# A layernorm feeding a diagonal state-space layer and a Mish MLP: the pipeline rebuilt around one PSUM accumulation, with B and C resident on chip, sine tables and one ring for the weights

## The chip, the core and the metric

The kernel runs on one core of one Trainium2 chip. The metric is the device time of one execution in microseconds (us), taken as the median of several runs; lower is better. In the text PE is the tensor engine (matmuls), DVE the vector engine, ACT the scalar engine (functions by table), POOL the general engine, SP the engine whose queue only issues transfers. Each engine works through its own instructions in order; semaphores tie them together.

## The reference, cut to what matters

```python
xn = layernorm(x)                                   # x: (2048, 1024), bf16
# A: a diagonal state-space layer with 1024 complex channels
dt = exp(log_dt);  Lam_bar = exp(dt * Lam)
Bu = xn @ (((Lam_bar - 1) / Lam)[:, None] * B).T    # complex, (2048, 1024)
h[t] = Lam_bar * h[t - 1] + Bu[t]                   # over the 2048 rows
yA = 2 * real(h @ C.T) + xn * Dskip
# B: a Mish MLP
u  = xn @ w1 + b1                                   # (2048, 3584)
yB = (u * tanh(log(1 + exp(u)))) @ w2               # softplus in the stable form
out = x + yA + yB
```

## The kernel before

The 2048 rows are cut into 4 blocks of 512. A block has four stretches of matmuls, each matmul 128 x 128 weights against 512 columns. `but_block` (the input projection): 8 channel groups j, each real and imaginary, 8 contraction steps k: 128 matmuls on line 761. `ffn1_block` (dense 1): 28 tiles f of 128 hidden units, 8 steps each: 224 matmuls on line 714. `tail_block`: dense 2, 28 tiles f into 8 PSUM banks (4 row tiles q times 2 column halves): 224 on line 801; then the output projection, 8 groups j, two parts, into the same banks: 128 on line 818.

The rows are normalized by DVE with one square root on ACT per row tile (`ln_tile` for block 0, lines 387 to 406, with two buffers; `mln_*` for the later blocks), stored to a scratch in DRAM (line 405 or 612) and read back transposed, eight transfers of 128 columns (`dma_xnT`, line 419). B is read transposed at the start, 16 transfers on SP (line 473) under one semaphore, so the first matmul waits for all of them. C is read transposed again in every block (`dma_rs`, line 463). w1 and w2 stream in every block through two sets of three slots (lines 443 and 452); a transfer waits on SP until PE has read the slot.

The recurrence is made a plain running sum: the projected input is multiplied by tables Wt that hold the inverse powers of Lam_bar (lines 767 to 778), summed along the row axis (lines 658 and 661), and multiplied by Vt, the powers with the factor of C (lines 681 to 692). The tables are built on DVE by nine doublings (lines 531 to 551); Vt is built in pieces between the bias adds of dense 1 in block 0 (`deferred`, lines 558 to 573). Four one-element instructions per group carry the state to the next block (lines 667 to 680).

Mish runs by groups of 7 tiles: DVE adds the bias out of PSUM (line 719), ACT does Exp, Ln and Tanh tile by tile (727, 732, 737) with table loads between, and POOL multiplies (739). POOL also loads row tiles of x and of the scratch again (626, 628) and forms x + xn * Dskip (634, 637); DVE adds that to the PSUM banks and ACT issues the stores (825 to 832).

What sets the order is the position in each engine's list, and for each instruction the waits that `_hazards` derives from the buffers it reads and writes. Block order in `build_kernel`: `but_block`, `ffn1_block`, `tail_block`.

## Time and profile before

| | us |
|---|---|
| runs, in order | 780.35, 2398.21, 777.31 |
| median of the runs | 780.35 |
| span of the profiled execution | 777.7 |
| granted clock of PE, mean over the span | 0.968 |
| PE busy, DVE busy | 627.5, 568.8 |
| ACT busy, POOL busy | 261.0, 274.0 |

The profiled execution is known by its span, from its first to its last instruction; what lies around it isn't shown for it, and the span lies between the two lower runs. One of the three runs took three times as long; the median leaves it aside.

How to read the profile: a row of a group gives line, engine, operation, the tile written and the tiles read, shapes and count, then the busy time and the mean duration (ns) of one, then how long the engine sat idle just before these instructions and what ended most of that. A row of the chain of waits or the timeline begins with the time from the span's start and a duration in us. A row of a stage gives for PE, the weight loads, DVE, ACT and POOL the busy us and the number of instructions, then PE's granted clock, the busy share of the DMA engines and GB/s. Matmuls are pipelined: their mean duration is longer than the time from one to the next.

### The profile page before, as it was taken

The numbers are of one execution on the slowest core, as the hardware profiler recorded it, in microseconds if no ns is written. First come the engines' busy times: TensorE is split into PE (matmuls) and PEld (weight loads), VectorE is DVE, ScalarE is ACT, GpSimd is POOL, SyncE is SP. The second block draws the span as 40 slices with busy tenths as digits, with TensorE's granted clock in tenths as the row PEclk, the third lists the DMA queues.
The fourth block names the chain that finished last, engine by engine and source line by source line (L and its number), as shares of the span: only waits on it lengthen the run. The fifth ranks groups of instructions, "written<-read, shape, count | busy, mean of one in ns | idle before, by whom it ended". The sixth has DMA issues, their size and how long they took to land.

```text
span 777.7 us, 8473 instructions
## 1 busy us (share of the span) xinstructions
PE 627.5 (81%) x2760; PEld 277.6 (36%) x2816; DVE 568.8 (73%) x1018; ACT 261.0 (34%) x415; POOL 274.0 (35%) x276
## 2 busy tenths in 40 slices
PE   0000999567998699898999787999999699999992
PEld 0000444223443244343444333444444244444441
DVE  2599999960599879738997289549995198479932
ACT  0250004599000000799400000999100005994000
POOL 0000000546344410146745310345664300567653
PEclk9999999997999899999999989999999999999997
DMA  4279014268568761454569913354669804514372
GB/s 55 75 176 168 0 55 139 79 189 191 194 228 180 150 142 55 136 148 123 181 216 171 211 62 108 110 152 145 206 171 179 169 8 137 160 60 172 116 144 81
DMA packets 193019, 105.70 MB, mean 136 GB/s; under 512 B 112464, under 2 KB 173904, under 8 KB 192976
## 3 DMA queue, kind: packets, MB, share of 16 engines
q1 hardware_dynamic: 183376, 86.28, 44.3%
q0 software_dynamic: 4992, 14.69, 6.9%
q10 hardware_dynamic: 4608, 4.20, 1.9%
q8 instruction: 23, 0.38, 0.2%
q14 instruction: 20, 0.16, 0.1%
HBM read 71.58 MB, written 8.39 MB: 103 GB/s over the span
## 4 chain that ended last, share of the span: by engine, by line
PE 26%; DVE 22%; DMA 16%; POOL 14%; ACT 12%; SPq 5%; issue 4%; POOLq 0%; DVEq 0%; ACTq 0%
PE bank L714 15%; DMA xntf<-bass_xn_scratch 11%; PE bank L761 8%; ACT actT L737 4%; POOL xdsk L634 4%; POOL actT L739 4%; POOL xdsk L637 4%; ACT actT L732 3%; SPq L473 3%; ACT actT L727 2%; DVE stats L590 2%; PE bank L801 2%; DVE hb L719 2%; DMA xl<-in_A_x_dram 2%; POOL xtf L626 2%
## 5 line engine op out<-in xcount | busy, mean ns | idle before, releaser
L739 POOL TENSOR_TENSOR actT<-hb,actT 128x512 bf16<-128x512 bf16 x112 | 141.8, 1301 | 357.3 <-ACT actT L737 324.2
L801 PE MATMUL bank<-w2s,actT 128*128 128x512 bf16 x880 | 199.7, 386 | 15.5 <-issue 6.1
L714 PE MATMUL bank<-xnT,w1s 128*128 128x512 bf16 x876 | 196.3, 381 | 19.3 <-DVE hb L719 18.3
L761 PE MATMUL bank<-xnT,BT 128*128 128x512 bf16 x504 | 117.8, 394 | 92.6 <-DMA BT<-in_A_B_im_dram 76.8
L727 ACT ACTIVATE actT<-hb 128x512 bf16<-128x512 bf16 x112 | 62.8, 618 | 330.2 <-DVE hb L719 329.7
L801 PEld LDWEIGHTS bank<-w2s,actT 128*128 128x128 bf16 x896 | 88.5, 99 | 126.4 <-issue 17.6
L714 PEld LDWEIGHTS bank<-xnT,w1s 128*128 128x128 bf16 x896 | 87.1, 98 | 127.9 <-issue 21.3
L719 DVE TENSOR_SCALAR hb<-bank,b1col 128x512 bf16<-128x512 f32 x112 | 81.0, 747 | 58.4 <-PE bank L714 40.6
L818 PE MATMUL bank<-rhs,hT 128*128 128x512 bf16 x500 | 115.5, 389 | 9.2 <-DVE hT L691 8.6
L761 PEld LDWEIGHTS bank<-xnT,BT 128*128 128x128 bf16 x512 | 51.1, 101 | 158.6 <-DMA BT<-in_A_B_im_dram 76.8
L634 POOL TENSOR_TENSOR xdsk<-xntf,dsk 128x512 bf16<-128x512 bf16 x32 | 42.5, 1328 | 104.1 <-DMA xntf<-bass_xn_scratch 104.1
L818 PEld LDWEIGHTS bank<-rhs,hT 128*128 128x128 bf16 x512 | 50.8, 100 | 73.2 <-DVE hT L691 10.6
L825 DVE TENSOR_TENSOR outs<-bank,xdsk 128x512 bf16<-128x512 f32 x32 | 20.9, 687 | 71.0 <-PE bank L818 32.0
L732 ACT ACTIVATE actT<-actT,consts 128x512 bf16<-128x512 bf16 x112 | 70.3, 708 | 0.2
L737 ACT ACTIVATE actT<-actT 128x512 bf16<-128x512 bf16 x112 | 60.0, 616 | 0.2
L637 POOL TENSOR_TENSOR xdsk<-xdsk,xtf 128x512 bf16<-128x512 bf16 x32 | 41.3, 1291 | 4.6
L661 DVE TENSOR_TENSOR_SCAN cum<-zeros,qb,hT 128x512 bf16<-128x512 bf16 x24 | 40.4, 1682 | 0.0
L590 DVE BATCH_NORM_STATS2 stats<-xl_60 128x6 f32<-128x512 bf16 x24 | 16.5, 689 | 32.5 <-DMA xl_60<-in_A_x_dram 32.1
L658 DVE TENSOR_TENSOR_SCAN cum<-zeros,qb,hT 128x512 bf16<-128x512 bf16 x24 | 34.2, 1426 | 0.0
L727 ACT ACT_TABLE_LOAD x3 | 3.8, 1283 | 71.1 <-PE bank L761 71.0
L767 DVE TENSOR_TENSOR mtmp<-bank,Wt 128x512 bf16<-128x512 f32 x32 | 22.1, 690 | 3.0
L773 DVE TENSOR_TENSOR mtmp<-bank,Wt 128x512 bf16<-128x512 f32 x32 | 22.1, 692 | 1.1
(113 smaller groups left out, 481.2 us busy)
## 6 DMA issues: line engine op xcount, KB each, us to landing
w1s<-in_B_w_dram SPq DMA_DIRECT2D x56, 512.0 KB, 3.8
w2s<-in_B_w_dram SPq DMA_DIRECT2D x56, 512.0 KB, 3.7
xtf<-in_A_x_dram POOLq DMA_DIRECT2D x32, 128.0 KB, 3.4
xntf<-bass_xn_scratch POOLq DMA_DIRECT2D x32, 128.0 KB, 3.5
out_dram<-outs ACTq DMA_DIRECT2D x32, 128.0 KB, 4.1
xl_60<-in_A_x_dram POOLq DMA_DIRECT2D x12, 256.0 KB, 4.7
bass_xn_scratch<-xnl_61 POOLq DMA_DIRECT2D x12, 256.0 KB, 5.0
xl<-in_A_x_dram SPq DMA_DIRECT2D x4, 256.0 KB, 2.7
```

Source lines behind the costliest of these rows:

```text
L634: pop(lambda e, bb_=bb_, xs=xs, u=u: e.tensor_tensor(xdsk[:, u, :], xntf[:, xs, :], dsk[:, bb_ * TB:(bb_ + 1) * TB], op=ALU.mult), reads=[ ...
L637: pop(lambda e, xs=xs, u=u: e.tensor_tensor(xdsk[:, u, :], xdsk[:, u, :], xtf[:, xs, :], op=ALU.add), reads=[b_xtf[xs], b_xdsk[u]], writes ...
L661: vop(lambda e, cim_=cim_, vim=vim, init_im=init_im: e.tensor_tensor_scan(out=cim_, data0=zeros[:], data1=vim, initial=init_im, op0=ALU.ad ...
L714: return e.matmul(banks[bank][:, :], lhsT=w1s[:, s_, k, fi * P128:(fi + 1) * P128], rhs=xnT[:, k, :], start=(k == 0), stop=(k == NK - 1))
L719: vop(lambda e, hs=hs, bank=bank, f=f: e.tensor_scalar(hb[:, hs, :], banks[bank][:, :], b1col[:, f:f + 1], None, op0=ALU.add), reads=[b_ba ...
L727: aop(lambda e, hs=hs, f=f: e.activation(actT[:, f, :], hb[:, hs, :], AF.Exp), reads=[b_hb[hs]], writes=[b_act[f]])
L732: aop(lambda e, ff=ff: e.activation(actT[:, ff, :], actT[:, ff, :], AF.Ln, bias=consts[:, 2:3], scale=1.0), reads=[b_act[ff], b_consts], w ...
L737: aop(lambda e, ff=ff: e.activation(actT[:, ff, :], actT[:, ff, :], AF.Tanh), reads=[b_act[ff]], writes=[b_act[ff]])
L739: pop(lambda e, hs2=hs2, ff=ff: e.tensor_tensor(actT[:, ff, :], hb[:, hs2, :], actT[:, ff, :], op=ALU.mult), reads=[b_hb[hs2], b_act[ff]], ...
L761: return e.matmul(banks[bk][:, :], lhsT=BT[:, ci, k, j * P128:(j + 1) * P128], rhs=xnT[:, k, :], start=(k == 0), stop=(k == NK - 1))
L801: return e.matmul(banks[u][:, :], lhsT=actT[:, f, q * P128:(q + 1) * P128], rhs=w2s[:, s_, fi, bb_ * TB:(bb_ + 1) * TB], start=first, stop ...
L818: return e.matmul(banks[u][:, :], lhsT=hT[:, ci, j, q * P128:(q + 1) * P128], rhs=rhs[:, s_, ci, bb_ * TB:(bb_ + 1) * TB], start=False, st ...
```

## The change

The kernel is written anew around the same four stretches of matmuls; the matmuls are as many and as large as before.

- Order in a block: dense 1, then the input projection, then dense 2 and the output projection in one accumulation (`tail`). The first 6 tiles of dense 2 go to banks 4 to 7 first. The last three groups of the output projection go row tile by row tile, so that the adds and stores of the first row tile begin before the last matmuls.
- Layernorm: x is loaded once, kept in `xx`; the normalized rows stay in `xn`. For block 0 they are transposed by PE into PSUM and copied out; for later blocks by transfers from on-chip memory (`transpose_dma`). The scratch in DRAM is gone. DVE forms x + xn * Dskip in place (`ln_skip`) and adds the PSUM banks to it.
- The recurrence uses the scan with a decay r = |Lam_bar| on DVE; the rotation is taken off before it and put on after it with cosine and sine tables (`tab`). Tables: POOL computes phases less whole turns, ACT takes Sin. Products work on real and imaginary parts in one instruction.
- B and C are read transposed once, during dense 1 of block 0, on SP, between the ring's loads; C is scaled by the channels' factor on ACT and DVE in block 0 (`scale_C`).
- w1 and w2 share one ring of 7 slots of 512 KB in the order of use.
- Mish: Exp, Ln and Tanh are one instruction for 7 tiles, and the product is one DVE instruction (`mish_mul`) in place of 7 on POOL.
- Parameter vectors are loaded row-wise by POOL and transposed by PE.

The core of the diff (the helper classes are rewritten too; waits are derived in the same way):

```diff
-    xn_scr = nc.dram_tensor("bass_xn_scratch", (S, D), bf16).ap()
-    NW2S = 3
-    w2s = sb("w2s", [P128, NW2S, 2, D], bf16); b_w2s = [Buf("w2s%d" % i) for i in range(NW2S)]
-    NRS = 4
-    NW1S = 3
-    w1s = sb("w1s", [P128, NW1S, NK, 256], bf16); b_w1s = [Buf("w1s%d" % i) for i in range(NW1S)]
...
+    NRING = 7
+    ring = sb("ring", [P, NRING, 2048], bf16)
+    CT = sb("CT", [P, 2, NJ, D], bf16)
...
+    ph = [scratch("ph_%s%d" % w, w[0], w[1], f32, TB)
+          for w in (("h", 2), ("h", 3), ("h", 6), ("h", 7), ("a", 11), ("a", 12), ("a", 13),
+                    ("h", 0), ("h", 1), ("h", 4), ("h", 5))]
...
-    def dma_xnT(c_):
-        for k in range(NK):
-            def fn(e, c_=c_, k=k):
-                return e.dma_start_transpose(xnT[:, k, :], xn_scr[c_ * TB:(c_ + 1) * TB, k * P128:(k + 1) * P128])
-            dma(fn, s_xnT, reads=[b_xnscr[c_ * NQ + q_] for q_ in range(NQ)], writes=[b_xnT])
...
-    def dma_rs(c_, j):
-        if c_ >= NB or (c_, j) in rs_done:
...
+    items = []
+    for blk in range(NB):
+        items += [("w1", g) for g in range(NF // 2)] + [("w2", g) for g in range(NF // 2)]
...
+        kind, g = items[i]
+        s = i % NRING
+        if kind == "w1":
+            dst = ring[:, s, :].rearrange("p (k f) -> p k f", k=NK)
+            src = B_w1[:, g * 256:(g + 1) * 256].rearrange("(k p) f -> p k f", p=P)
...
+    def ln_stats(blk, q):
+        i, s = blk % 2, q % 2
+        for h in range(2):
+            vop(lambda e, h=h: e.bn_stats(stats[:, s, h, :], xx[:, i, q, h * 512:(h + 1) * 512]),
...
+        aop(lambda e: e.activation(rs[:, q, 1:2], rs[:, q, 0:1], AF.Sqrt), reads=[b_rs[q]], writes=[b_rs[q]])
+    def ln_apply(blk, q):
+        i = blk % 2
...
+        vop(lambda e: e.tensor_scalar(xn[:, q, :], xx[:, i, q, :], mv[:, q, 0:1], y,
+                                      op0=ALU.subtract, op1=ALU.mult),
+    def ln_skip(blk, q):
+        i = blk % 2
...
+        vop(lambda e: e.tensor_tensor(m, xn[:, q, :], dsk[:], op=ALU.mult),
...
+        vop(lambda e: e.tensor_tensor(xx[:, i, q, :], xx[:, i, q, :], m, op=ALU.add),
...
+    def transpose_dma(q):
+        SP.dma(lambda e: e.dma_start_transpose(xnT[:, :, q * P:(q + 1) * P], xn[:, q, :]),
...
+    for q in range(NQ):
+        ln_stats(0, q)
+        if q:
+            ln_apply(0, q - 1)
+    ln_apply(0, NQ - 1)
+    for q in range(NQ):
+        for k in range(NK):
+            PE.mm(lambda e, q=q, k=k: e.transpose(ps16(q)[:, k * P:(k + 1) * P], xn[:, q, k * P:(k + 1) * P], ident[:]),
...
+        if q < NQ - 1:
+            aop(lambda e, dst=dst, srcp=srcp: e.copy(dst, srcp), reads=[b_ps[q]], writes=[b_xnT[q]])
+        else:
+            vop(lambda e, dst=dst, srcp=srcp: e.tensor_copy(dst, srcp), reads=[b_ps[q]], writes=[b_xnT[q]])
...
-    for i_ in range(LOGT):
-        L_ = 1 << i_
-        ur_b = up[:, 0, i_, :].unsqueeze(2).to_broadcast([P128, NJ, L_])
-        ui_b = up[:, 1, i_, :].unsqueeze(2).to_broadcast([P128, NJ, L_])
-        vop(lambda e, L_=L_, ur_b=ur_b: e.tensor_tensor(p_re[:, :, L_:2 * L_], p_re[:, :, 0:L_], ur_b, op=ALU.mult),
-            reads=[b_pre, b_up[i_][0]], writes=[b_pre])
...
+    def phases(j):
+        for s in range(2):
+            dst, b_dst = ph_slot(j, s)
+            turn = 0.25 if s == 0 else 0.0
+            pop(lambda e, turn=turn: e.tensor_scalar(px[:], iot[:], cj("thp", j), turn, op0=ALU.mult, op1=ALU.add),
...
+            pop(lambda e: e.tensor_scalar(py[:], px[:], ROUND_MAGIC, ROUND_MAGIC, op0=ALU.add, op1=ALU.subtract),
...
+            pop(lambda e, dst=dst: e.tensor_tensor(dst[:], px[:], py[:], op=ALU.subtract),
...
+    def table(j):
+        for s in range(2):
+            src, b_src = ph_slot(j, s)
+            aop(lambda e, s=s, src=src: e.activation(tab[:, s, j, :], src[:], AF.Sin, scale=TWO_PI, bias=kon[:, 1:2]),
...
+    def coefficients():
...
+        aop(lambda e: e.activation(c("s1"), c("xs"), AF.Sin, scale=TWO_PI, bias=kon[:, 1:2]),
...
+    for j in range(NJ):
+        if j == 5:
+            break
+        phases(j)
...
+    def scale_C(j):
+        for h in range(D // HB):
...
+            aop(lambda e, ta=ta, cim=cim: e.activation(ta[:], cim, AF.Copy, scale=cj("nci2", j)),
...
+            vop(lambda e, ta=ta, cre=cre: e.scalar_tensor_tensor(
+                out=cre, in0=cre, scalar=cj("cr2", j), in1=ta[:], op0=ALU.mult, op1=ALU.add),
...
+    def transpose_B(j):
+        for ci, src in enumerate((A_B_re, A_B_im)):
+            SP.dma(lambda e, ci=ci, src=src: e.dma_start_transpose(BT[:, ci, j, :, :], src[j * P:(j + 1) * P, :]),
...
+    def transpose_C(i):
+        ci, db = i % 2, i // 2
+        src = (A_C_re, A_C_im)[ci]
+        SP.dma(lambda e: e.dma_start_transpose(CT[:, ci, :, db * P:(db + 1) * P], src[db * P:(db + 1) * P, :]),
...
+    def mish(g):
...
+        aop(lambda e: e.activation(a, hs, AF.Exp), reads=[b_hb[g % 2]], writes=[b_act[g]])
+        aop(lambda e: e.activation(a, a, AF.Ln, bias=1.0), reads=[b_act[g]], writes=[b_act[g]])
+        aop(lambda e: e.activation(a, a, AF.Tanh), reads=[b_act[g]], writes=[b_act[g]])
...
+    def mish_mul(g):
+        hs = hb[:, (g % 2) * GF:(g % 2) * GF + GF, :]
+        a = act[:, g * GF:(g + 1) * GF, :]
+        vop(lambda e: e.tensor_tensor(a, a, hs, op=ALU.mult), reads=[b_act[g], b_hb[g % 2]], writes=[b_act[g]])
...
+    def first_tile(f):
...
+        for k in range(NK):
...
+        if fi == 1:
+            item_done()
+        if f % GF == 0 and f >= 2 * GF:
+            mish_mul(f // GF - 2)
+        vop(lambda e: e.tensor_scalar(hb[:, hs, :], ps[:, bank, :], b1(f), None, op0=ALU.add),
+            reads=[b_ps[bank], b_par], writes=[b_hbf[hs]])
+        if f % GF == GF - 1:
+            mish(f // GF)
...
-            vop(lambda e, m1=m1, pr=pr, j=j: e.tensor_tensor(m1, banks[pr][:, :], Wt[:, 0, j, :], op=ALU.mult),
...
+                for k in range(NK):
+                    PE.mm(lambda e, j=j, ci=ci, k=k, bank=bank: e.matmul(
+                        ps[:, bank + ci, :], lhsT=BT[:, ci, j, k, :], rhs=xnT[:, k, :], start=k == 0, stop=k == NK - 1),
+                        reads=[b_BT[j]] + b_xnT, writes=[b_ps[bank + ci]], first=k == 0, last=k == NK - 1)
+            u = ps[:, bank:bank + 2, :]
+            for s in range(2):
+                vop(lambda e, s=s, u=u, j=j: e.tensor_tensor(
+                    mt[:, s, :, :], u, tab[:, s, j, :].unsqueeze(1).to_broadcast([P, 2, TB]), op=ALU.mult),
...
+            vop(lambda e, j=j: e.tensor_tensor(hT[:, 0, j, :], mt[:, 0, 0, :], mt[:, 1, 1, :], op=ALU.add),
...
+            vop(lambda e, j=j: e.tensor_tensor(hT[:, 1, j, :], mt[:, 0, 1, :], mt[:, 1, 0, :], op=ALU.subtract),
...
+            if j == 2:
+                mish_mul(2)
+            if j == 6:
+                mish_mul(3)
...
-        vop(lambda e, cre=cre, vre=vre, init_re=init_re: e.tensor_tensor_scan(
-            out=cre, data0=zeros[:], data1=vre, initial=init_re, op0=ALU.add, op1=ALU.add),
...
+    def recur(blk, j):
+        for ci in range(2):
+            init = 0.0 if blk == 0 else qi[:, ci, j:j + 1]
+            vop(lambda e, ci=ci, init=init: e.tensor_tensor_scan(
+                out=hT[:, ci, j, :], data0=cj("r", j).to_broadcast([P, TB]), data1=hT[:, ci, j, :], initial=init,
+                op0=ALU.mult, op1=ALU.add),
...
+        for s in range(2):
+            vop(lambda e, s=s: e.tensor_tensor(
+                mt[:, s, :, :], hT[:, :, j, :], tab[:, s, j, :].unsqueeze(1).to_broadcast([P, 2, TB]), op=ALU.mult),
...
+        vop(lambda e: e.tensor_tensor(hT[:, 0, j, :], mt[:, 0, 0, :], mt[:, 1, 1, :], op=ALU.subtract),
...
+        vop(lambda e: e.tensor_tensor(hT[:, 1, j, :], mt[:, 0, 1, :], mt[:, 1, 0, :], op=ALU.add),
...
-                    pop(lambda e, hs2=hs2, ff=ff: e.tensor_tensor(actT[:, ff, :], hb[:, hs2, :], actT[:, ff, :], op=ALU.mult),
...
-        for u in range(NU):
-            dma_unit_tiles(c_, u)
-            xdsk_prep(u)
...
+        base = n_item[0]
+        for f in range(6):
+            dense(f, (base + f // 2) % NRING, (4, 5, 6, 7))
+        for f in range(NF):
+            dense(f, (base + f // 2) % NRING, (0, 1, 2, 3) if f < 6 else range(8))
+            if f % 2 == 1:
+                item_done()
+            if blk + 1 < NB and f in (7, 9, 11, 13):
+                transpose_dma((f - 7) // 2)
+        for j in range(NJ - NJT):
+            for ci in range(2):
+                for u in range(8):
+                    proj(j, ci, u, False)
+        i = blk % 2
+        for q in range(NQ):
+            for j in range(NJ - NJT, NJ):
+                for ci in range(2):
+                    for u in (2 * q, 2 * q + 1):
+                        proj(j, ci, u, j == NJ - 1 and ci == 1)
+            xr = xx[:, i, q, :]
+            vop(lambda e, q=q, xr=xr: e.tensor_tensor(
+                xr, ps[:, 2 * q:2 * q + 2, :].rearrange("p a t -> p (a t)"), xr, op=ALU.add),
+                reads=[b_ps[2 * q], b_ps[2 * q + 1], b_xx[i][q]], writes=[b_xx[i][q]])
+            r0 = blk * TB + q * P
+            out_events[i, q] = AC.dma(lambda e, xr=xr, r0=r0: e.dma_start(out[0, r0:r0 + P, :], xr), s_out[i][q],
+                                      reads=[b_xx[i][q]])
+        if blk + 2 < NB:
+            for q in range(NQ):
+                load_x(PO, blk + 2, q)
...
+    for blk in range(NB):
+        def side(f):
+            if blk == 0:
+                if f == 0:
+                    for q in range(NQ):
+                        ln_skip(0, q)
+                if f == 1:
+                    ln_stats(1, 0)
+                    ln_stats(1, 1)
+                    ln_apply(1, 0)
+                    ln_stats(1, 2)
+                    ln_apply(1, 1)
...
+                    coefficients()
+                if f == GF - 1:
+                    for j in range(5):
+                        table(j)
+                    for j in range(5, NJ):
+                        phases(j)
+                if f == 3 * GF - 1:
+                    for j in range(5, NJ):
+                        table(j)
+                if f < 16 and f % 2 == 0:
+                    transpose_B(f // 2)
+                if f >= 16:
+                    transpose_C(f - 16)
+        for f in range(NF):
+            first_tile(f)
+            side(f)
+        if blk == 0:
+            for i in range(12, 2 * NK):
+                transpose_C(i)
+        project_in(blk)
+        if 0 < blk < NB - 1:
+            for q in range(NQ):
+                ln_stats(blk + 1, q)
+                if q:
+                    ln_apply(blk + 1, q - 1)
+            ln_apply(blk + 1, NQ - 1)
+        for j in range(NJ):
+            recur(blk, j)
+            if blk == 0:
+                scale_C(j)
+        if blk + 1 < NB:
+            carry()
+            for q in range(NQ):
+                ln_skip(blk + 1, q)
+        tail(blk)
+    SP.wait(out_events.values())
```

1045 lines of the change are left out of this document (347 added, 698 removed).

## The prediction

> **What bounds the kernel now.** I read four views in this order: the page's busy shares and slices, the stages with their granted clock, the waits of the engines, and the chain that ended last. All times are us after the span's start.
>
> ```profile
> PE 627.5 (81%) x2760; PEld 277.6 (36%) x2816; DVE 568.8 (73%) x1018; ACT 261.0 (34%) x415; POOL 274.0 (35%) x276
> ...
> PE   0000999567998699898999787999999699999992
> ```
> ```profile
> 0.00:76.80 76.80, 0.00 (x0) 0.00 (x0) 51.75 (x160) 18.38 (x29) 1.71 (x12) 1.00 0.60 120
> ...
> 160.00:195.00 35.00, 24.68 (x90) 10.07 (x93) 7.79 (x12) 33.77 (x55) 21.00 (x19) 0.82 0.78 196
> ...
> 640.00:688.00 48.00, 47.74 (x220) 21.72 (x222) 29.42 (x46) 36.72 (x58) 15.66 (x14) 1.00 0.42 121
> ```
> ```profile
> PE bank L761 <- DMA BT<-in_A_B_im_dram: 76.8, 1, 76.8
> ...
> PE bank L714 <- DVE hb L719: 18.3, 12, 4.5
> ```
> ```profile
> 641.37 10.74 PE bank L714 x49
> ...
> 758.70 2.33 DMA xntf<-bass_xn_scratch
> 761.11 1.16 POOL xdsk L634
> ```
>
> PE is the engine with most work, and it is idle 777.7 - 627.5 = 150 us. Half of that is the head: no matmul before 76.8, because the first matmul (L761) waits for the last transposed tile of B. The rest lies in block 0 (the stage 160 to 195: PE 24.7 of 35 us, ACT busy throughout, clock 0.82) and at the end of each block, where the chain runs through loads of normalized rows and POOL's skip products, not PE. Where nothing holds it, PE does 49 matmuls in 10.74 us, 0.219 us each, at clock 1.00. The kernel has 704 matmuls of that size in each of 4 blocks (224 + 128 + 224 + 128), and the change keeps them all: 154.3 us a block, 617 in all. That is the floor under what follows.
>
> **The durations that I use.**
>
> ```profile
> L739 POOL TENSOR_TENSOR actT<-hb,actT 128x512 bf16<-128x512 bf16 x112 | 141.8, 1301 | 357.3 <-ACT actT L737 324.2 <-DVE xnl_61 L609 13.2 <-DVE hb L719 12.2
> ...
> L719 DVE TENSOR_SCALAR hb<-bank,b1col 128x512 bf16<-128x512 f32 x112 | 81.0, 747 | 58.4 <-PE bank L714 40.6 <-POOL actT L739 14.3 <-ACT actT L727 1.4
> L732 ACT ACTIVATE actT<-actT,consts 128x512 bf16<-128x512 bf16 x112 | 70.3, 708 | 0.2
> L727 ACT ACTIVATE actT<-hb 128x512 bf16<-128x512 bf16 x112 | 62.8, 618 | 330.2 <-DVE hb L719 329.7
> ...
> L661 DVE TENSOR_TENSOR_SCAN cum<-zeros,qb,hT 128x512 bf16<-128x512 bf16 x24 | 40.4, 1682 | 0.0
> ...
> L767 DVE TENSOR_TENSOR mtmp<-bank,Wt 128x512 bf16<-128x512 f32 x32 | 22.1, 690 | 3.0
> ...
> L737 ACT ACT_TABLE_LOAD x16 | 20.5, 1283 | 0.3
> ...
> L771 DVE TENSOR_TENSOR hT<-mtmp 128x512 bf16<-128x512 bf16 x32 | 13.6, 425 | 1.1
> ...
> L658 DVE TENSOR_TENSOR_SCAN cum<-zeros,hT 128x512 bf16<-128x512 bf16 x8 | 9.7, 1217 | 0.0
> ...
> L560 DVE SCALAR_TENSOR_TENSOR tmp_58<-tmp_56,cs,tmp_58 128x512 f32<-128x512 f32 x8 | 6.8, 847 | 0.3
> ...
> L526 ACT ACTIVATE tmp_52<-tmp_54,cs 128x512 bf16<-128x512 f32 x8 | 5.8, 719 | 0.2
> ...
> L605 DVE TENSOR_TENSOR rstd_t<-rstd_t 128x1 f32<-128x1 f32 x12 | 1.9, 159 | 0.4
> ...
> L481 ACT ACTIVATE cs<-cs 128x8 f32<-128x8 f32 x1 | 0.2, 209 | 0.5 <-DVE cs L478 0.5
> ```
> ```profile
> L683 DVE TENSOR_TENSOR mtmp<-cum,Vt x32: 409/418/1379, 217.7 to 743.9; 128x512 bf16<-128x512 bf16 x32
> ...
> L670 DVE SCALAR_TENSOR_TENSOR qb<-cum,cs,qb x24: 218/819/1015, 216.8 to 587.8; 128x1 f32<-128x1 bf16 x24
> ```
>
> Longer forms follow from two sizes. A DVE product of bf16 tiles costs 0.16 + 0.52 ns x elements (L605, L771): 0.69 us for 1,024, 2.0 for 3,584. From PSUM it is 0.69 for 512 (L767), so about 1.22 for 1,024. An ACT function costs 0.21 + 0.81 ns x elements (L481, L727): 3.1 us for 3,584, and the logarithm by L732 3.8.
>
> **Head: T0, the first matmul.** Removed: the scratch in DRAM, eight transposes of it, and the wait for all of B. Kept: the layernorm of 512 rows. Added: 32 PE transposes and four copies out of PSUM. DVE now begins with the parameters: four small POOL loads, landing in about the 3.4 us of other POOL loads, a PE transpose, an exponential and three small products, done at about 8.5.
>
> ```profile
> 10.26 1.42 DVE L390 BATCH_NORM_STATS2 stats<-xl 128x6 f32<-128x512 bf16 x2 [10.26 <-DMA xl<-in_A_x_dram]
> ...
> 12.38 0.16 DVE L397 RECIPROCAL rstd_t<-rstd_t 128x1 f32<-128x1 f32 x1 [0.27 <-ACT rstd_t L396]
> ...
> 13.35 0.55 DVE L402 TENSOR_SCALAR xnl<-xl,mv,rstd 128x1024 bf16<-128x1024 bf16 x1
> ```
> ```profile
> xtf<-in_A_x_dram POOLq DMA_DIRECT2D x32, 128.0 KB, 3.4
> ```
>
> One tile takes 10.26 to 13.90, less the 0.27 for ACT, which the next tile's statistics now cover: 3.3, four of them 13. POOL meanwhile computes phases for the sine tables (`phases`, 30 instructions, then 18), which today's POOL does not do at that time. L683 shows what a busy POOL does to DVE: 0.42 us alone, up to 1.38 beside L739, and even the tiny L670 goes from 0.22 to 0.82. So DVE instructions with two SBUF inputs, or the wide scaling of L402, wait some 0.85 each for POOL; twelve in this stretch would be 10, bounds 0 and 12 x 1.3 = 16. I take 8, since two of three phase instructions have one input. The transposes and the last copy (1.22) add 2.5. T0 = 8.5 + 13 + 8 + 2.5 = 32, bounds 24 and 40. All seven ring loads are issued by then.
>
> The Trainium skill (SBUF — State Buffer, "Who interferes with whom") calls the port pair of VectorE and GpSimd an exclusive lock, so that the later instruction blocks until the earlier ends. By that rule each of the twelve pays a whole POOL instruction, and T0 would be an estimated 4 to 8 us later, toward my upper bound; the 1.38 above agrees with it.
>
> **Block 0, in us after T0.** PE needs 154.3; the rest is waiting.
> - *DVE queue.* `side(0)` and `side(1)` put the skip products (8 x 0.69), block 1's layernorm (13) and 24 coefficient steps with a Sin load (5.5) ahead of the bias add of tile 2. That is 24, with 6 for the lock 30, from 2.5 on. The add of tile 2 ends at 34. PE, with 8 banks, comes to tile 10 at 17.5 and needs that bank: it waits 16.5.
> - *ACT queue.* A group of 7 tiles is Exp 3.1, Ln 3.8, Tanh 3.1 and two table loads, 12.5; after a Sin one load more, 13.8. The first starts at 37.5 (bias 6) and ends at 51. Five tables (10 x 0.72 + 1.3) end at 60, group 1 at 73.5, group 2 at 86, three tables at 91.5, group 3 at 105.5.
> - *DVE again.* Bias 21 to 27 stands behind the product of group 1 and ends at 81; the input projection is 2 x 1.22 + 2 x 0.43 = 3.3 for each of 8 channels plus two group products of 2.0, and it waits for group 3 before its last channel: 111.5. Only then are PSUM banks 2 and 3 free for dense 2, of which PE has done 24 matmuls (5.3) by that time. PE has then done 49 + 28 + 5.3 = 82.5 in 111.5: 29 lost, the 16.5 among them.
> - *Recurrence and C.* Per channel two scans, two wide and two narrow products, 4.7, and in this block four scalings of C at about 0.8 (L560, its undisturbed form being shorter): 7.8 x 8 = 62, done at 174. PE has 43.8 of dense 2 and 17.5 of projection left, and comes to the last channel at 174.6. It is just covered; 1 us more per channel would show as 8.
> - *Cold clock.* After a stall the matmuls are slower:
>
> ```profile
> 254.76 3.63 PE L818 MATMUL bank<-rhs,hT 128*128 128x512 bf16 x16 [2.15 <-DVE hT L691]
> 261.64 6.50 PE L818 MATMUL bank<-rhs,hT 128*128 128x512 bf16 x16 [3.25 <-DVE hT L691]
> ```
>
> The second costs 2.9 more. I take 3 for block 0.
>
> Block 0 = 154.3 + 29 + 3 = 186, bounds 160 (the queues cover one another) and 205.
>
> **Blocks 1 to 3.** POOL then only issues four loads, so DVE runs undisturbed. DVE needs 21 (bias) + 8 + 26.4 + 13 + 37.6 + 1.2 + 5.5 + 5 = 118 of the 154. ACT needs 4 x 12.5 + 1.3. DVE ends a block's recurrence at 83 + 13 + 37.6 = 134 after the block's start (83 being the end of its input projection, 3.3 x 8 + 4 from 52.5), and PE comes to the last channel at 49 + 28 + 49 + 17.5 = 144. SP loses the re-reads of C, and the ring asks for 512 KB per 16 matmuls, 150 GB/s; between 640 and 688 the queues moved 121 GB/s at a DMA share of 0.42, so there is room. The transposes of normalized rows have some 50 us of dense 2 and projection as cover; without it they cost their landing, 2.8 us by the row below. PE waits about 0.6 for banks 2 and 3. I take 155 each, 465; bounds 154 and 161 (scans at the 1.68 of their slower group, 16 x 0.46 = 7).
>
> ```profile
> xnT<-bass_xn_scratch SPq DMA_TRANSPOSE x32, 2.8
> ```
>
> **End.**
>
> ```profile
> 763.76 0.38 PE L818 MATMUL bank<-rhs,hT 128*128 128x512 bf16 x1
> ...
> 772.85 0.17 DVE L869 TENSOR_SCALAR cs<-cs 128x8 f32<-128x8 f32 x1 [1.87 <-DMA out_dram<-outs]
> ```
> ```profile
> xl<-in_A_x_dram SPq DMA_DIRECT2D x4, 256.0 KB, 2.7
> ```
>
> Last add 1.3, a 256 KB store 3 to 4, and 777.7 - 773.0 = 4.7 after the last instruction: 10.
>
> **Sum.** 32 + 186 + 465 + 10 = 693 as a span. The profiled span of before, 777.7, lies between the runs 777.31 and 780.35, the latter being the median; half of that 2.7 is added: 695.
>
> **Rivals.**
> - *A, the first block is covered* (0.16): POOL rarely blocks DVE and ACT's chain hides. T0 24, block 0 167, 465, 10: 666, with the offset 667. For it: the median of L683 is 0.42, though POOL works beside it at times. Against: the wait at tile 10 needs no lock; 24 us of DVE work alone is more than the 15 of bank cover.
> - *B, POOL is worse* (0.2): every phase instruction takes the 1.3 of L739. T0 40, the stall 8 longer, phases 5 to 7 hold group 2 by another 8: 40 + 202 + 465 + 10 = 717, time 718.
> - *C, transposes hold SP in block 0* (0.09): 28 of them stand between the ring loads.
>
> ```profile
> 49.14 3.62 SPq L473
> ...
> 57.32 1.30 SPq L473
> ```
> ```profile
> 48.02 1.08 SPq L443 DMA_DIRECT2D w1s<-in_B_w_dram  x1
> ```
>
> At 1.30 each they and 14 loads at 1.08 take 52 us of SP against 66 of dense 1 and the ring's lead of 24. At 3.62 they take 116 against 90: 26 later, 721.
> - *D, slower than before* (0.04): a PE with hardly a gap is granted less clock. At 0.82, as from 160 to 195, the matmuls take 617/0.82 = 752, time 830. It decides from 617/(617 + 85) = 0.88 down. Against it: 48 us without a gap from 640 on ran at 1.00, and the low clocks stand beside gaps.
>
> The forecast has 0.5, and its own range is 677 to 712. The remaining 0.01 is a change that does not keep PE fed, within 2% of before.
>
> **How the numbers follow.** Measurement of this kernel tells about 2% from no change: 764.7 to 796. Forecast, A, B and C are all below: faster 0.95. Same 0.01, slower 0.04. The range goes from A to a little above B and C, 664 to 728; below it I leave 0.08, above 0.11.
>
> **What would show it.** The head: first matmul of dense 1 at about 32, after transposes. The pile: PE waiting for a bias add at tile 10 for 16 us, DVE without a gap before it. ACT: four fused groups of about 12.5 us. Block 0 ends near 218, later blocks repeat every 155 with clock 1.00 and no waits for the ring. I am wrong if blocks 1 to 3 are far above 155, which would mean DVE or DMA, not PE, is the bound, or if block 0 is far from 186.

## The result, and the profile after

The changed kernel takes 679.39 us (median of 4 runs, 678.09 to 680.35) against 778.83 of the kernel before on the same chip (median of 4, one of them 2398.21): ratio 0.8795, interval 0.872 to 0.8871. Ratios, here and below, are taken over the fast runs of both kernels, of which the one before also has slower ones, so they need not be the quotients of the medians. The forecast was 695, range 664 to 728. The profiled execution has a span of 676.4.

Four lines of the page of the kernel after: PE's busy time, its slices, its clock, and the shares of the chain that ended last.

```profile
PE 621.5 (92%) x2849; PEld 280.4 (41%) x2849; DVE 478.6 (71%) x718; ACT 247.7 (37%) x163; POOL 74.9 (11%) x74
...
PE   0583979999968999999999999999999999999997
...
PEclk9995999999997999999999999999999999999999
...
PE 73%; DVE 17%; ACT 7%; issue 1%; DMA 1%; POOL 0%; DVEq 0%; ACTq 0%; POOLq 0%
```

PE's row has gaps only in its first third; from the 14th slice on it is full, up to the last. The timeline of PE says where they lie (start, duration, line, what, count, and in brackets the idle time before it and what ended it):

```profile
27.47 19.99 PE L526 MATMUL ps<-xnT,ring 128*128 128x512 bf16 x80 [0.99 <-DVE xnT L411]
61.84 33.69 PE L526 MATMUL ps<-xnT,ring 128*128 128x512 bf16 x144 [14.38 <-issue]
...
101.64 27.41 PE L546 MATMUL ps<-xnT,BT 128*128 128x512 bf16 x120 [4.38 <-DVE hb L533]
128.88 48.51 PE L602 MATMUL ps<-ring,act 128*128 128x512 bf16 x224
...
196.86 1.04 PE L602 MATMUL ps<-CT,hT 128*128 128x512 bf16 x4 [1.34 <-DVE CT L487]
205.69 11.01 PE L602 MATMUL ps<-CT,hT 128*128 128x512 bf16 x40 [7.80 <-DVE CT L487]
216.53 48.51 PE L526 MATMUL ps<-xnT,ring 128*128 128x512 bf16 x224
...
368.48 48.51 PE L526 MATMUL ps<-xnT,ring 128*128 128x512 bf16 x224
...
644.75 27.79 PE L602 MATMUL ps<-CT,hT 128*128 128x512 bf16 x128
```

Dense 1 of a block begins with L526 and the block's last matmuls are L602 with CT. So block 0 runs from 27.47 to 216.53. Blocks 1 and 2 take 151.95 each to the hundredth, and block 3, from 520.43 to the end of its last matmul at 672.5, takes 152.1; there is no wait in them. The same view of the kernel before:

```profile
76.84 29.22 PE L761 MATMUL bank<-xnT,BT 128*128 128x512 bf16 x126 [76.84 <-DMA BT<-in_A_B_im_dram]
...
272.14 27.79 PE L761 MATMUL bank<-xnT,BT 128*128 128x512 bf16 x126
...
736.35 27.79 PE L818 MATMUL bank<-rhs,hT 128*128 128x512 bf16 x125
```

The two spans differ by 101.3, and the stages account for it:

| stage | before | after | gained |
|---|---|---|---|
| head, to the first large matmul | 76.8 | 27.5 | 49.4 |
| block 0 | 195.3 | 189.1 | 6.2 |
| blocks 1 to 3 | 492.0 | 456.0 | 36.0 |
| after the last matmul | 13.6 | 3.9 | 9.7 |

The ends of blocks are the starts of the next, the last being the end of the last matmul. Half of the gain is the head. Block 0 gained least: a block without waits takes 152, and it takes 37 more. 27.9 of these are the four waits in the brackets above (14.38, 4.38, 1.34, 7.80); the rest is mostly matmuls at half speed, at the block's start and after the three longer waits (last section).

### The profile page after: what moved, and what is told of

It is laid out like the page before. It is cut to its first block, busy times and chain, and to the rows that moved or that the text cites. A ratio compares the mean times of both kernels' runs of the same rounds, so it can differ in the third digit from the quotient of the medians.

```text
span 676.4 us, 7254 instructions
## 1 busy us (share of the span) xinstructions
PE 621.5 (92%) x2849; PEld 280.4 (41%) x2849; DVE 478.6 (71%) x718; ACT 247.7 (37%) x163; POOL 74.9 (11%) x74
## 4 chain that ended last, share of the span: by engine, by line
PE 73%; DVE 17%; ACT 7%; issue 1%; DMA 1%; POOL 0%; DVEq 0%; ACTq 0%; POOLq 0%
PE ps L602 35%; PE ps L526 22%; PE ps L546 16%; DVE hT L566 3%; DVE CT L487 2%; DVE CT L484 2%; DVE stats L337 2%; DVE mt L571 2%; ACT tab L428 1%; DVE xn L354 1%; ACT act L508 1%; ACT act L506 1%; ACT act L507 1%; ACT ct L480 1%; DMA st<-in_B_b_dram 1%
## 5 line engine op out<-in xcount | busy, mean ns | idle before, releaser
L526 PE MATMUL ps<-xnT,ring 128*128 128x512 bf16 x896 | 199.2, 386 | 15.4 <-issue 14.4
L602 PE MATMUL ps<-ring,act 128*128 128x512 bf16 x896 | 194.0, 379 | 0.0
L526 PEld LDWEIGHTS ps<-xnT,ring 128*128 128x128 bf16 x896 | 88.7, 99 | 125.1 <-issue 22.4
L533 DVE TENSOR_SCALAR hb<-ps,par 128x512 bf16<-128x512 f32 x112 | 81.8, 749 | 75.5 <-PE ps L526 74.7
L602 PEld LDWEIGHTS ps<-ring,act 128*128 128x128 bf16 x896 | 87.7, 98 | 105.7
L602 PE MATMUL ps<-CT,hT 128*128 128x512 bf16 x512 | 113.7, 384 | 9.1 <-DVE CT L487 9.1
L546 PE MATMUL ps<-xnT,BT 128*128 128x512 bf16 x512 | 112.7, 382 | 4.4 <-DVE hb L533 4.4
L551 DVE TENSOR_TENSOR mt<-ps,tab 128x1024 bf16<-128x1024 f32 x64 | 75.3, 1219 | 11.4 <-PE ps L546 9.9
L602 PEld LDWEIGHTS ps<-CT,hT 128*128 128x128 bf16 x512 | 50.5, 99 | 71.7 <-DVE CT L487 10.1
L566 DVE TENSOR_TENSOR_SCAN hT<-cs,qi,hT 128x512 bf16<-128x512 f32 x48 | 58.9, 1269 | 0.0
L507 ACT ACTIVATE act<-act 128x3584 bf16<-128x3584 bf16 x16 | 51.0, 3190 | 0.2
L508 ACT ACTIVATE act<-act 128x3584 bf16<-128x3584 bf16 x16 | 51.0, 3190 | 0.2
L420 POOL TENSOR_SCALAR py<-px 128x512 f32<-128x512 f32 x16 | 31.1, 1944 | 1.4
```

The lines of the kernel that those rows point to most:

```text
L420: pop(lambda e: e.tensor_scalar(py[:], px[:], ROUND_MAGIC, ROUND_MAGIC, op0=ALU.add, op1=ALU.subtract), reads=[b_px], writes=[b_py])
L507: aop(lambda e: e.activation(a, a, AF.Ln, bias=1.0), reads=[b_act[g]], writes=[b_act[g]])
L508: aop(lambda e: e.activation(a, a, AF.Tanh), reads=[b_act[g]], writes=[b_act[g]])
L526: PE.mm(lambda e, k=k: e.matmul(ps[:, bank, :], lhsT=wt[:, k, fi * P:(fi + 1) * P], rhs=xnT[:, k, :], start=k == 0, stop=k == NK - 1), rea ...
L533: vop(lambda e: e.tensor_scalar(hb[:, hs, :], ps[:, bank, :], b1(f), None, op0=ALU.add), reads=[b_ps[bank], b_par], writes=[b_hbf[hs]])
L546: PE.mm(lambda e, j=j, ci=ci, k=k, bank=bank: e.matmul(ps[:, bank + ci, :], lhsT=BT[:, ci, j, k, :], rhs=xnT[:, k, :], start=k == 0, stop= ...
```

## The experiments

All edits but those of `e8_bhoist` and `e9_skiplead` are made in the changed kernel, or in a version of it that is named; ratios are to the kernel before, timed beside each, and gains are against the 679.39.

**More scratch for the scaling of C (`e1_ct6`).** PE waits 9.1 for L487, the scaling of C, and DVE there waits 11.8 for ACT. I first took the ring of three scratch tiles for the cause.

```diff
-    for i in range(3):
+    NCT = 6
+    for i in range(NCT):
...
-            ta, b_ta = ct[n_ct[0] % 3]
+            ta, b_ta = ct[n_ct[0] % NCT]
```

> The new kernel with six scratch tiles for the scaling of C instead of three. Theory: in block 0 each channel group of the recurrence takes 8.84 us on DVE, of which 1.47 is a wait for ACT, which itself could not write the third scratch tile before DVE had read the first; with six tiles ACT runs ahead, a group takes about 7.4 to 7.8, DVE ends the last group some 8 to 11 us earlier, the two waits of PE for C (1.3 and 7.8) shrink to under 2, and the time falls by 8 to 10 from 679. Rival: ACT is late for another reason (it starts a group's copies only when DVE has finished the group before), then the wait stays and the time stays within 2 us.

Measured: 678.9 (678.27 to 679.41), 0.8717 [0.8663, 0.8771]: nothing. The waits of the changed kernel and then of this run (a row gives the sum, the count, the longest):

```profile
DVE CT L484 <- ACT ct L482: 11.8, 8, 1.5
PE ps L602 <- DVE CT L487: 9.1, 2, 7.8
```
```profile
DVE CT L485 <- ACT ct L483: 11.8, 8, 1.5
PE ps L603 <- DVE CT L488: 8.9, 2, 7.8
```

The same waits, within 0.2. The scratch alone wasn't what ACT waited for; that theory fell.

**The pile on DVE dealt out (`e2_spread`).** Skip products, block 1's layernorm and the coefficients go one at a time behind the bias adds of tiles 0 to 16, in place of all behind tiles 0 and 1.

```diff
-                if f == 0:
-                    for q in range(NQ):
-                        ln_skip(0, q)
-                if f == 1:
-                    ln_stats(1, 0)
...
+                if f < 4:
+                    ln_stats(1, f)
+                if f == 4:
+                    coefficients()
+                if f == 7:
+                    coefficients2()
+                if 8 <= f < 12:
+                    ln_skip(0, f - 8)
+                if f in (12, 13, 15, 16):
+                    ln_apply(1, (12, 13, 15, 16).index(f))
```

> The new kernel with the work that stands on DVE before the bias add of tile 2 in block 0 (skip products, block 1's layernorm, coefficients) dealt out over tiles 0 to 16 of dense 1. Theory that the pile makes the stall: PE's wait of 14.4 at tile 10 goes, the first group of Mish starts near 46 instead of 64, ACT's four groups end near 113 instead of 130, and block 0 shortens by 14 to 19, to a time of 660 to 665. Rival, that ACT's chain or the recurrence sets the end of block 0 whatever the pile: the wait moves to the start of dense 2 or to the output projection, and the time falls by under 5.

Measured: 660.34 (658.88 to 661.31), 0.8483 [0.8415, 0.8551]; 19 us less. PE's timeline:

```profile
27.96 40.67 PE L527 MATMUL ps<-xnT,ring 128*128 128x512 bf16 x176 [0.99 <-DVE xnT L411]
71.13 12.15 PE L527 MATMUL ps<-xnT,ring 128*128 128x512 bf16 x48 [2.50 <-issue]
83.11 27.79 PE L547 MATMUL ps<-xnT,BT 128*128 128x512 bf16 x128
```

The stop behind 80 matmuls is gone, and with it the wait before the input projection; a shorter one of 2.50 stands in dense 1. It was order, not work: every instruction is still there.

**POOL's phases without their work (`e3_nophase`).** POOL writes a constant where it computed the phases, so the rotation is left out.

```diff
-            pop(lambda e, turn=turn: e.tensor_scalar(px[:], iot[:], cj("thp", j), turn, op0=ALU.mult, op1=ALU.add),
...
+            pop(lambda e, dst=dst: e.memset(dst[:], 0.25), writes=[b_dst])
```

> The new kernel without the phases: POOL writes a constant where it computed the phases of the sine tables, so the rotation is left out of the recurrence and all else is as it was. Theory that POOL's reads hold DVE's two-input instructions: a row tile of the first layernorm takes 3.3 instead of 4.14, the first matmul of dense 1 comes near 24 instead of 27.5, the pile ahead of tile 2 shortens from 31 to about 24, and with it all that follows in block 0: time lower by 8 to 11. Rival, that DVE's own work is the whole of it: under 2 lower.

Measured: 671.09 (670.83 to 672.32), 0.862 [0.8566, 0.8674]; 8.3 less. The wait behind 80 matmuls fell from 14.38 to 6.82, so POOL's presence made 7.6 of it. The first matmul came at 26.93, hardly earlier. The timelines of DVE and POOL in this run say why:

```profile
9.97 3.27 DVE L388 TENSOR_SCALAR cs<-cs 128x8 f32<-128x8 f32 x1
```
```profile
8.00 1.94 POOL L418 MEMSET ph_h<- 128x512 f32 x4
...
11.26 1.94 POOL L418 MEMSET ph_h<- 128x512 f32 x4
```

POOL's writes, eleven in a row that end at 13.20, hold a DVE instruction of 128x8 until 13.24, for 3.27 us, where it took 0.17 in the changed kernel. Without that artefact the head would have been an estimated 3 shorter; so this run is a flawed measure of the head, and a fair one of the wait.

**Spread and scratch together (`e4_both`).**

> Both edits, the six scratch tiles and the dealt-out pile. If the two losses lie behind one another on the path, the gains add: 22 to 28 lower than 679, near 654. If the second edit only uncovers what the first had hidden, the gain is that of the larger one, 14 to 19.

Measured: 659.51 (659.43 to 659.95), 0.8469 [0.8418, 0.8521]: as `e2_spread`. The scratch adds nothing here either.

**The scaling of C in another order (`e5_reorder`).** Six scratch tiles, and the four copies on ACT stand ahead of the four scalings on DVE. In the code as it is, the second half's copies read the buffer CT[j] that the first half's scaling writes (both halves are one buffer where the waits are derived).

```diff
         for h in range(D // HB):
...
             aop(lambda e, tb=tb, cre=cre: e.activation(tb[:], cre, AF.Copy, scale=cj("nci2", j)),
                 reads=[b_CT[j], b_cs["nci2"]], writes=[b_tb])
+            todo.append((cre, cim, ta, b_ta, tb, b_tb))
+        for cre, cim, ta, b_ta, tb, b_tb in todo:
             vop(lambda e, ta=ta, cre=cre: e.scalar_tensor_tensor(
```

> In block 0 the four ACT copies of a channel group's C are issued ahead of the four DVE scalings, into a ring of six scratch tiles; as the kernel stands, ACT's copies of the second half of C wait until DVE has written the first half, because both halves are one buffer to the tracker (the wait of ACT on DVE's scaling, 8 times). New theory, after more scratch tiles alone brought nothing: this queue order makes DVE wait 1.47 us per group for ACT (11.8 us over 8) and PE 9.1 us for the scaled C. Then the wait of DVE on ACT's copies falls below 2 us in all, PE's wait for the scaled C below 2, block 0 ends 8 to 9 earlier and the time is 668 to 672. Rival: DVE's own work per group (two scans, six products, four scalings) is what PE waits for; then the waits of DVE move elsewhere and the time is 677 to 681.

Measured: 667.66 (667.16 to 668.51), 0.8603 [0.8555, 0.865]; 11.7 less. The output projection of block 0 now runs through, and DVE's row of waits for ACT's copies is gone from the view:

```profile
178.89 27.79 PE L605 MATMUL ps<-CT,hT 128*128 128x512 bf16 x126
```

9.1 were the waits, and most of the rest is the slow start behind the longer one (2.2, last section), which goes too.

**Both orders (`e6_best`).**

> Both at once: layernorm, skip products and coefficients of block 0 dealt out among the bias adds, and the reordered scaling of C. Theory: the two waits lie one behind the other in block 0, so the gains add: 19 from the pile and 8 to 9 from C, 650 to 653. Rival: with the pile gone DVE reaches the recurrence no earlier than ACT lets it, or PE runs into the next wait (transposes of C, the ring); then 656 to 661.

Measured: 648.45 (648.04 to 648.76), 0.8355 [0.8301, 0.841]. The gains add: 19.0 and 11.7 are 30.7, the run shows 30.9.

**The Mish product back on POOL (`e7_mulpool`).** One part of the change undone.

```diff
-        vop(lambda e: e.tensor_tensor(a, a, hs, op=ALU.mult), reads=[b_act[g], b_hb[g % 2]], writes=[b_act[g]])
+        for t in range(GF):
+            pop(lambda e, t=t: e.tensor_tensor(a[:, t, :], a[:, t, :], hs[:, t, :], op=ALU.mult),
+                reads=[b_actf[g * GF + t], b_hbf[(g % 2) * GF + t]], writes=[b_actf[g * GF + t]])
```

> One part of the change undone: the Mish product runs on POOL again, tile by tile, 28 instructions per block, in place of four wide ones on DVE. Theory: blocks 1 to 3 are bound by PE with cover on every side, and POOL at 1.3 us per product keeps pace with PE's 1.74 per tile; they stay at 151.95 each, within 1. Only block 0 may change, where POOL's phases stand ahead of the products; total 674 to 690. Rival: beside a POOL that works on on-chip tiles, DVE's products and scans take up to 1.85 times as long (0.22 to 0.82 and 0.42 to 1.38 were seen before), which eats the 30 to 40 us that DVE has to spare per block; then blocks 1 to 3 take 156 to 165 each and the total is 692 to 720.

Measured: 690.88 (688.34 to 691.48), 0.8894 [0.8843, 0.8946]. The stage of block 1, changed kernel first, then this run (length, then busy us and count of PE, weight loads, DVE, ACT, POOL, then clock, DMA share, GB/s):

```profile
216.53:368.48 151.95, 151.95 (x705) 68.88 (x704) 110.97 (x166) 50.31 (x25) 2.73 (x5) 1.00 0.42 120
```
```profile
226.79:378.73 151.94, 151.20 (x691) 68.91 (x704) 107.64 (x162) 50.32 (x25) 35.61 (x34) 1.00 0.42 120
```

Later blocks don't notice where the product runs. All of the loss is in block 0, which ends 10 later, with a second wait of 14.31 in dense 1, because POOL's products stand behind its phases. So in the steady state this part of the change bought nothing; its worth is in block 0. No row shows the rival's 1.85: beside POOL a product with both inputs on chip took up to 1.38 in place of 0.42 (last section), and the later blocks had the time to spare.

**B early in the kernel before (`e8_bhoist`).** Twelve of the sixteen transposed reads of B go into the time in which SP waits for the layernorm.

```diff
     def ln_tile(rt, dmaeng=None):
...
+        for i in range(3 * rt, 3 * rt + 3):
+            dma_bt(i)
...
```

> In the kernel before: twelve of the sixteen transposed reads of B are issued between the layernorm's transfers on SP, where SP waits for DVE anyway, and only four behind the loads of w1. Nothing else changes. Theory: the early PE start is worth nothing by itself there, since DVE's tables, done at 84.7, and then its projection products without a gap to 113.7 are the next wall; the first matmul comes at 55 to 62 in place of 76.8, PE then waits for DVE at the banks, DVE's first product of the projection stays at 84 to 86, and the time stays within 4 us of before (776 to 784). Rival: the arrival of B is what the head of before costs, and its gain passes through: 760 to 768.

Measured: 781.95 (772.92 to 786.77) against 778.33 (760.99 to 782.69), 1.0182 [1.0086, 1.0279]: no gain. PE's timeline, then DVE's:

```profile
60.30 15.30 PE L766 MATMUL bank<-xnT,BT 128*128 128x512 bf16 x63 [60.30 <-DMA BT<-in_A_B_im_dram]
88.25 16.66 PE L766 MATMUL bank<-xnT,BT 128*128 128x512 bf16 x63 [12.64 <-DVE mtmp L778]
```
```profile
81.10 4.42 DVE L554 SCALAR_TENSOR_TENSOR Wt<-tmp,tmp 128x4096 bf16<-128x4096 bf16 x1
```

PE starts 16.5 earlier, fills its banks and waits for DVE, whose table ends at 85.5 (84.8 in the kernel before); dense 1 begins at 104.75, only 1.2 earlier than before. The longest wait of the kernel before, 76.8 for B, had a second one of nearly the same length behind it.

**Loads of the skip product ahead, in the kernel before (`e9_skiplead`).**

```diff
-        for u in range(NU):
+        for u in range(NXT):
             dma_unit_tiles(c_, u)
+        for u in range(NU):
             xdsk_prep(u)
+            if u + NXT < NU:
+                dma_unit_tiles(c_, u + NXT)
```

> In the kernel before: in every block POOL issues the loads of four units of the skip product ahead, in place of load, wait, product for each unit (104 us of POOL waiting for those loads). Theory: what the change won in blocks 1 to 3 beyond the matmuls (158.4, 170.4 and 162.3 there against 151.95) is mostly this chain: PE waits 5.5 and 7.0 for the adds of the block before, and the bias adds and the end come late behind it. Then these waits fall below 1.5 each, blocks 2 and 3 end up at 158 or less, the tail after the last matmul shrinks by 2 to 5, and the time falls by 12 to 20 (758 to 767 beside a before of 778). Rival: the adds wait for something else (DVE's own queue, PSUM, the transposed rows), and the time stays within 5 of before.

Measured: 768.42 (766.65 to 774.64), 0.9872 [0.9819, 0.9925]; 8.6 less, between the two theories. The waits of PE for the adds are gone and the tail after the last matmul fell from 13.6 to 5.8. But blocks 0 and 1 grew, by 5.6 and 6.9. One of the recurrence's products and PE's wait behind the recurrence, first in the kernel before, then here:

```profile
L687 DVE TENSOR_TENSOR mtmp<-cum,Vt 128x512 bf16<-128x512 bf16 x32 | 18.6, 581 | 1.1
...
PE bank L818 <- DVE hT L691: 8.6, 4, 3.3
```
```profile
L687 DVE TENSOR_TENSOR mtmp<-cum,Vt 128x512 bf16<-128x512 bf16 x32 | 27.9, 873 | 1.1
...
PE bank L821 <- DVE hT L691: 19.9, 9, 6.5
```

POOL's products, no longer spread out by their loads, come some 4 apart in place of 7, beside DVE's recurrence, whose instructions grow longer; a good part of the gain is given back there.

**Statistics ahead of the parameters (`e10_early`, on `e6_best`).**

```diff
+    ln_stats(0, 0)
+    ln_stats(0, 1)
     PE.op(lambda e: e.transpose(ps16(7)[:, 0:NST], st[:, :], ident[0:NST, 0:NST]),
...
-        ln_stats(0, q)
-        if q:
-            ln_apply(0, q - 1)
-    ln_apply(0, NQ - 1)
+        ln_apply(0, q)
+        if q + 2 < NQ:
+            ln_stats(0, q + 2)
```

> On the best version: the statistics of the first two row tiles go ahead of the parameters on DVE, which is idle until 8.8; their rows are there at about 5. Theory: the head is DVE's queue from 8.8 on, so the 3.5 us of work that is moved ahead comes off it, less what POOL's phases take back and one more table load on ACT (1.28); first matmul of dense 1 at 25 to 26 in place of 27.7, time 645 to 647. Rival: the row tiles go in step with POOL's cycle of 4.14, whatever DVE has to do in it; then the first matmul stays at 27 to 28 and the time at 648.

Measured: 651.94 (650.82 to 652.76), 0.8363 [0.8305, 0.842]. The first matmul did come 3.5 earlier, at 24.21; the time is 3.5 longer. ACT's wait for POOL in this run, then PE's timeline where dense 2 goes on, first here and then in `e6_best`:

```profile
ACT act L511 <- POOL ph_a L423: 5.3, 1, 5.3
```
```profile
117.50 45.75 PE L607 MATMUL ps<-ring,act 128*128 128x512 bf16 x194 [4.69 <-DVE mt L556]
```
```profile
116.12 42.91 PE L606 MATMUL ps<-ring,act 128*128 128x512 bf16 x194 [1.27 <-DVE mt L555]
```

ACT's third Mish group writes over POOL's scratch, and POOL, which works on phases without a gap, ends at 81.75; in `e6_best` it ended at 80.37 and ACT waited 0.43. So dense 2 goes on 1.4 later, and after the longer wait the same matmuls take 2.8 more: together the 4.2 by which block 0 ends later (190.71 against 186.49).

**One channel group's phases to DVE (`e11_phase7`, on `e10_early`).**

```diff
-                    for j in range(5, NJ):
+                    for j in range(5, NJ - 1):
                         phases(j)
+                if f in (18, 19):
+                    phase_dve(NJ - 1, f - 18)
...
```

> On the run before, in which the first matmul came 3.5 earlier and the time was 3.5 longer: the two phase tables of the last channel group are computed by DVE, behind the bias adds of tiles 18 and 19, so that POOL has 6 instructions (8.3 us) less. Theory: block 0 hangs on POOL, which works on phases without a gap from 10 to 82, and ACT's third Mish group waits 5.3 us for POOL's last phase, because it writes over POOL's scratch; then that wait falls below 1, the wait of PE of 4.7 in dense 2 below 1, and the time is 643 to 647. Rival: ACT's own chain of groups and tables, or DVE, which gets some 4 us more work in its fullest stretch, holds block 0; then 649 to 654.

Measured: 644.04 (643.84 to 645.78), 0.8302 [0.824, 0.8363]: the fastest version, 35 us below the changed kernel. ACT's wait for POOL is gone, and block 0 runs from 23.53 to 182.30, 158.8, as long as in `e6_best`; what it gains over that run is nearly all the earlier start. The row behind block 0:

```profile
182.30 48.51 PE L545 MATMUL ps<-xnT,ring 128*128 128x512 bf16 x224
```

## Why the prediction was right, and where its sizes were off

| term | forecast | measured |
|---|---|---|
| head | 32 | 27.5 |
| block 0 | 186 | 189.1 |
| blocks 1 to 3 | 465 | 456.0 |
| end | 10 | 3.9 |
| span | 693 | 676.4 |

The direction, the bound and the place and size of the largest wait were right. The 16.6 that the sum is too high come from three sizes; block 0 was 3 too low.

*The pitch of a matmul* is the largest. The 0.219 is a row's length over its count, 10.74 over 49; but a row runs to the end of its last matmul, and one alone is 0.38 long (the kernel before, at 352.77), more than the time from one start to the next. From the start of dense 1 of block 1 to that of its input projection, 216.53 to 264.88, 224 matmuls take 48.35, 0.2158 each, and 48 of these and 0.38 are just the 10.74. A block is then 151.95 in place of 154.3, 7.0 less over blocks 1 to 3; the other 2 of their 9.0 are the 0.7 a block for small waits that did not come. The Trainium skill (TensorE: Matmul & The Clock Gate, "Wait — 56ns, not 53.3ns?") gives 215.7 ns from start to start at 512 columns once the array is warm; the trace agrees.

*The end* was charged with the 4.7 that the kernel before has behind its last instruction. Here an add (1.23) and a store (2.0 to landing, by the page) nearly fill the 3.9.

*The head* was charged too much for the lock. Forecast 13 of layernorm and 8 of lock; from 9.66 to 25.39 it took 15.7. The lock is real but smaller:

```profile
14.86 0.94 DVE L354 TENSOR_SCALAR xn<-xx,mv,rs 128x1024 bf16<-128x1024 bf16 x1
...
17.66 0.53 DVE L349 SCALAR_TENSOR_TENSOR rs<-rs 128x1 f32<-128x1 f32 x1
...
18.41 0.56 DVE L353 TENSOR_TENSOR rs<-rs 128x1 f32<-128x1 f32 x1
19.00 0.94 DVE L354 TENSOR_SCALAR xn<-xx,mv,rs 128x1024 bf16<-128x1024 bf16 x1
...
24.82 0.57 DVE L354 TENSOR_SCALAR xn<-xx,mv,rs 128x1024 bf16<-128x1024 bf16 x1
```
```profile
14.90 1.92 POOL L420 TENSOR_SCALAR py<-px 128x512 f32<-128x512 f32 x1
16.91 1.26 POOL L422 TENSOR_TENSOR ph_h<-px,py 128x512 f32<-128x512 f32 x1
18.27 0.69 POOL L418 TENSOR_SCALAR px<-iot,cs 128x512 f32<-128x512 f32 x1
19.05 1.92 POOL L420 TENSOR_SCALAR py<-px 128x512 f32<-128x512 f32 x1
```

DVE's scaling comes every 4.14, as POOL's cycle of three instructions does; where POOL does nothing (`e3_nophase`) the tiles are 3.05 apart. The two engines go in step, at 1.09 a tile for three tiles: an estimated 3.3 of lock. The two small instructions with two inputs pay 0.31 and 0.40 (0.22 and 0.16 alone): L349 ends at 18.19 and L353 at 18.97, just as POOL's L422 (18.17) and L418 (18.96) do. L418 has one input tile, so the forecast's reason for less lock, that two of the three phase instructions have one input, does not hold; the price of 0.85 was too high. The scaling pays 0.37 (0.94 against the 0.57 of the last row); that row ran beside POOL's L420 too, so what holds it isn't shown.

*Block 0*, step by step. PE stopped after 80 matmuls, which is tile 10, and waited 14.4 (forecast 16.5). The page calls that wait "issue"; the timeline of DVE gives the cause, and `e2_spread` shows it:

```profile
31.75 0.94 DVE L362 TENSOR_TENSOR mt<-xn,dsk 128x1024 bf16<-128x1024 bf16 x1
...
60.91 0.17 DVE L388 TENSOR_SCALAR cs<-cs 128x8 f32<-128x8 f32 x1
60.99 6.01 DVE L533 TENSOR_SCALAR hb<-ps,par 128x512 bf16<-128x512 f32 x9
```

The pile ends at 61.0, and the bias add that PE needs stands first behind it. The pile is 29.2 long where 30 was forecast, 24 of work and 6 of lock; in `e3_nophase` it is 21.9, which leaves 7.3 for the lock. ACT's chain, forecast to end at T0 + 105.5, ended at T0 + 102.4. The forecast then had PE wait 12.5 for banks 2 and 3. No such wait came: DVE had read them at 134.2, and PE, held up before, came to them at about 134.5. In its place PE waited 4.38 ahead of the input projection, where the bias adds of tiles 21 to 27 stood behind the product of group 1, and that behind ACT. The slow start was forecast as 3 and is about 9. The recurrence with the scaling of C was "just covered; 1 us more per channel would show as 8": a group took 8.84 in place of 7.8, 1.47 of it the wait of DVE for ACT, and PE waited 7.80 + 1.34. I had summed DVE's work and left out the hand-over between the two halves; `e5_reorder` shows that it was that.

So the total of block 0, 186 against 189.1, owes its closeness to luck. Up to the 24th matmul of dense 2 the forecast was 4.9 too long (111.5 after T0 against 106.6), and from there on 7.7 too short (74.8 against 82.5).

*Rivals.* A, block 0 covered, did not come, though the two reorderings of `e6_best` bring it to 158.8, within 7 of the matmuls. B's price of a POOL instruction (1.3) is right, the mean of the three is 1.3, but in the head's rows no DVE instruction pays a whole one. C and D: no wait for the ring appears, and the clock is 1.00 in every block without gaps.

*The head's gain of 49* was credited to the removal of the transposes of B and of the scratch. `e8_bhoist` shows that B alone was worth nothing; the tables on DVE, to 85, lay behind it. What of the 49 is owed to the sine tables and what to dense 1 coming first wasn't tried. Nor are the 36 of blocks 1 to 3 separated. In the kernel before, 27 of them are waits in PE's timeline, 13.2 of these for the adds that end the block before; `e9_skiplead`, which removes the waits for the adds, gets 8.6 back in all, and `e7_mulpool` rules out the product on POOL as such.

## What to carry to other kernels

The longest wait of a profile says what ends last, not what it is worth: look for the second wait that ends just behind it before you price the first. Work that another engine waits for should stand in a queue by its due time: dealing out a pile of 29 us behind the first 17 bias adds won 19 us with every instruction kept. Two halves of a tile that are one buffer where waits are derived make two engines take turns; and an earlier start wins nothing where another engine's chain, here POOL's phases, sets the end.
